# Dilated attention values as [v, ones, v] in gate stages, with one unit and several scores moved

## The chip, the cores and the metric

The kernel runs on one core of a Trainium2 chip. The metric is the device time of one execution in microseconds (us), as the median over several executions.

## The reference

Eight batches of eight heads, 576 positions, 64 elements a head. Heads 0 to 3 attend to the last 32 positions, heads 4 to 7 to every fourth of the last 128. The result is fed through a gated feed-forward block of 4608 tokens. This cut and the later ones are shortened: `...` stands for what is left out, and some comments are mine.

```python
def _attn_ref(q, k, v):
    window, dilation, scale = 32, 4, 1.0 / np.sqrt(D)
    scores = scale * np.matmul(q, k.transpose(0, 1, 3, 2))
    rel = pos[:, None] - pos[None, :]
    mask_plain = (rel >= 0) & (rel < window)
    mask_dil = (rel >= 0) & (rel < window * dilation) & (rel % dilation == 0)
    # heads 0 to 3 take mask_plain, heads 4 to 7 mask_dil
    ...
    attn = attn / (np.sum(attn, axis=-1, keepdims=True) + 1e-09)
    return np.matmul(attn, v)

def _moe_ref(x, w_gate, w_val, w_out):            # x: 4608 x 512
    g = x @ w_gate                                # 512 x 1536
    gelu = 0.5 * g * (1.0 + erf(g * inv_sqrt2))
    return gelu * (x @ w_val) @ w_out             # 1536 x 512
```

## The kernel before

The tokens go through the feed-forward block in 9 chunks of 512. A chunk is a gate stage, 12 blocks `nb` of 8 matmuls (`ffn1`), and an output stage, 4 blocks `tb` of 12 matmuls (`ffn2`). The attention of later batches is put between these matmuls. Its unit is a pair of heads of one batch: unit n belongs to batch n // 4, and units 22, 23, 26, 27, 30 and 31 are the dilated ones of batches 5 to 7. A unit consists of scores (TensorE), an exponential (ScalarE), a mask (VectorE), values (TensorE) and a normalization (VectorE). All of it goes through the four PSUM banks (PSUM is the memory that TensorE writes its results to) that the feed-forward matmuls leave free at that time.

The schedule is four tables. `values_a` puts the values of a unit behind block nb of a gate stage. `values_b` lists the units whose values go into an output stage, and `places` says where: "1.3v" is before matmul 3 of block 1, with s for a score, m for a mask, v for values and x for the normalizing multiply. One score also ends each gate stage of chunks 1 to 5.

```python
scores = {1: range(8, 12), 2: range(12, 17), 3: range(17, 22), 4: range(22, 27), 5: range(27, 32)}
values_b = {1: range(8, 12), 2: range(12, 16), 3: range(17, 20), 4: range(22, 24), 5: range(27, 28)}
values_a = {3: {4: 16}, 4: {2: 20, 6: 21}, 5: {1: 24, 4: 25, 7: 26}, 6: {1: 28, 4: 29, 7: 30, 10: 31}}
places = {
    ...
    2: "0.0m 1.3v 1.3s 1.3x 1.3m 2.5v 2.5s 2.5x 2.5m 3.0s 3.0m 3.6v 3.6x 3.7s 3.12w 3.12m",
    3: "0.0m 1.3v 1.3s 1.3x 1.3m 2.5v 2.5s 2.5x 2.5m 2.11s 2.11m 3.4s 3.6v 3.6x 3.6m",
    4: "0.0m 1.3v 1.3s 1.3x 1.3m 2.4v 2.4s 2.4x 2.4m 2.11s 2.11m 3.7s 3.7m",
    5: "0.0m 1.3v 1.3s 1.3x 1.3m 2.1s 2.1m 2.10s 2.10m 3.6s 3.6m",
}
```

A plain unit in a gate stage uses value tiles in which a block of ones lies between the values of two heads. A 128-column slice [v, ones] or [ones, v] then gives the numerator of a head in one half of the partitions and its denominator in the other half, with full-width matmuls. The price is on VectorE: the two heads lie in different banks and different halves, so each step of the normalization is done twice on 64 partitions.

```python
def emit_both(n, b0):                       # plain units in gate stages
    for hl in range(2):
        for j in range(5):
            trio = vp[:, j, hp] if j < 4 else vt[:, hp]          # [v, ones, v]
            nc.tensor.matmul(ps[:, b0 + 2 * hl + j // 4, ...],
                             trio[:, hl : hl + 2, :].rearrange("p x d -> p (x d)"), pt[:, hl, p0 : p0 + w], ...)

def norm_both_x(n, b0):
    for hl in range(2):
        half = slice(64 * hl, 64 * hl + 64)
        nc.vector.tensor_tensor(xT[pair(n)][half, ...], both_rows(hl, b0, hl), rb[half], ALU.mult)
```

A dilated unit, wherever it stands, takes the other form (`emit_pv`). Its denominators (ones as weights) and its numerators are separate half-width matmuls, and one transpose and one multiply on 128 partitions normalize it. The multiply also puts the four classes of positions back in order, by a permuted access pattern:

```python
num = ps[:, b0 + flip : b0 + flip + 2, 0 : 2 * NCL].rearrange("p s (m i) -> p i m s", m=2)
nc.vector.tensor_tensor(dst.rearrange("p (i m s) -> p i m s", m=2, s=2), num,
                        rb.rearrange("p (s m i) -> p i m s", s=2, m=2), ALU.mult)
```

The dilated values of a batch come in three DMAs on the software queue of GpSimd (`load_v_dil`). The keys and queries of a plain pair come through transposing DMAs into `qTp`. Chunk c loads those of batch c + 2, and their first score can stand in the same chunk: unit 28, the first of batch 7, has its score in chunk 5.

The softmax here doesn't subtract the row's maximum and nothing guards it: scores larger than these inputs give would overflow.

Of the kernel before, what the change touches and what calls it, by code (L numbers as in the profile page):

```python
# [21 lines left out]
def kernel(  # L22
# [10 lines left out]
    nc = tc.nc  # L33
# [23 lines left out]
    psum = ctx.enter_context(tc.tile_pool(name="psum", bufs=1, space=bass.MemoryType.PSUM))  # L57
    ldp = ctx.enter_context(tc.tile_pool(name="ldp", bufs=1))
    qtp = ctx.enter_context(tc.tile_pool(name="qtp", bufs=2))
    prb = ctx.enter_context(tc.tile_pool(name="prb", bufs=8))  # L60
    nrm = ctx.enter_context(tc.tile_pool(name="nrm", bufs=2))
    ffn = ctx.enter_context(tc.tile_pool(name="ffn", bufs=3))
    osbp = ctx.enter_context(tc.tile_pool(name="osbp", bufs=4))
# [11 lines left out]
    wo_t = [const.tile([P, 4, DM], F16, tag=f"wo{i}", name=f"wo{i}") for i in range(3)]  # L75
    xT = [const.tile([P, NT], F16, tag=f"xT{i}", name=f"xT{i}") for i in range(NKC)]

    HP = HK // 2
    vset = [
        (  # L80
            const.tile([P, 4, HP, 3, D], F16, tag=f"vp{i}", name=f"vp{i}"),
            const.tile([P, HK, 4, D], F16, tag=f"vd{i}", name=f"vd{i}"),
            const.tile([P, HP, 3, D], F16, tag=f"vt{i}", name=f"vt{i}"),
            const.tile([P, HK, 2, D], F16, tag=f"vr{i}", name=f"vr{i}"),
        )
        for i in range(3)
    ]
# [57 lines left out]
    def load_wo(i):  # L145
        return nc.gpsimd.dma_start(
            out=wo_t[i], in_=moe_w_out[i * CH : (i + 1) * CH, :].rearrange("(fc p) m -> p fc m", p=P)
        )

    tiles = {}  # L150
    gate = {}

# [9 lines left out]
    def fl(t):  # L162
        return t.rearrange("p h r d -> p h (r d)")
# [23 lines left out]
    def new_v(b):  # L187

        sv = ldp.tile([P, 5, HK, D], F32, tag="sv", name=f"sv{b}")
        tiles["v", b] = vset[b % 3]  # L190
        return sv

    def v_plain(b, sv, eng):
        for kb in range(5):
# [38 lines left out]
    def load_eights(b):  # L233
# [4 lines left out]
            )  # L238
        return q8

    def load_v_dil(b):
        nc.gpsimd.dma_start(out=fl(tiles["v", b][1]), in_=quads(v, b, HK, 0, 4 * P))
        load_v_dil_rest(b)

    def load_v_dil_rest(b):
        for m in range(2):
            nc.gpsimd.dma_start(
                out=fl(tiles["v", b][3][64 * m : 64 * m + 64]),
                in_=quads(v, b, HK, S - 256, S)[:, :, 2 * m * D : 2 * m * D + 2 * D],
            )  # L250

    def load_batch_plain(b):
        st = load_qk_plain(b)
# [31 lines left out]

    def is_plain(n):
        return pair(n) < NHP // 2

    def copy(eng, dst, src):
        if eng == "act":  # L290
# [105 lines left out]
    def emit_pv(n, b0, parts=("den", "num"), wide=False, flip=False):  # L396



        b, hp = n // NHP, n % 2  # L400
        vp, vd, vt, vr = tiles["v", b]
        pt = tiles["P", n]
        mms = []

        def add(hl, c0, dims, lhs, p0, pdims, st):

            base = ps[64 * hl : 64 * hl + 64, b0 + c0 // 512, c0 % 512 : c0 % 512 + 1]
            o = bass.AP(tensor=base.tensor, offset=base.offset, ap=[base.ap[0]] + dims)
            rhs = bass.AP(tensor=pt.tensor, offset=pt.offset + p0, ap=[pt.ap[0]] + pdims)
            mms.append((o, lhs, rhs, st))  # L410

        def run(n):
            return [[1, n]]

        if is_plain(n):
            if "den" in parts:
                d0 = 1024 if wide else 0 if flip else 960

                groups = (
                    ((0, 0, 4, P), (P, P, 3, 32), (PH - PT, 512, 1, PT))  # L420
                    if wide or flip
                    else ((0, 0, 1, 64), (64, 64, 1, 64), (PW, P, 3, P), (P, P, 3, 32), (PH - PT, 512, 1, PT))
                )
                for i, (p0, q0, runs, w) in enumerate(groups):
                    for hl in range(2):
                        st = i == 0 or i == (2 if wide or flip else 1)
                        add(hl, d0 + q0, [[P, runs], [1, w]], ones[:, 0:D], hl * PH + p0, [[PW, runs], [1, w]], st)
            if "num" in parts:
                for j in range(5):
                    for hl in range(2):  # L430
                        lhs = vp[:, j, hp, 2 * hl, :] if j < 4 else vt[:, hp, 2 * hl, :]
                        w = (PW, PW, PW, P, PT)[j]
                        p0 = hl * PH + j * PW - (32 if j == 4 else 0)
                        if not flip:
                            add(hl, j * P, run(w), lhs, p0, run(w), j in (0, 4))
                        elif j > 0:
                            add(hl, 960 + j * P, run(w), lhs, p0, run(w), False)
                        else:
                            add(hl, 960, run(64), lhs, p0, run(64), True)
                            add(hl, 1024, run(PW - 64), lhs, p0 + 64, run(PW - 64), True)  # L440
        else:
            if "den" in parts:

                groups = (
                    ((0, 0, DW, 1024), (1, 0, DW, 1536))
                    if wide
                    else ((0, 0, 192, 288), (0, 192, 96, 800), (1, 0, 96, 896), (1, 96, 192, 1312))
                )
                for i, (s, c, w, c0) in enumerate(groups):
                    for hl in range(2):  # L450
                        add(hl, c0, run(w), ones[:, 0:D], (2 * s + hl) * DW + c, run(w), wide or i != 2)
            if "num" in parts:
                for s in range(2):
                    for m in range(3):
                        for hl in range(2):
                            h, p0 = 2 * hp + hl, (2 * s + hl) * DW
                            if m < 2:
                                lhs, c0 = vd[:, h, 2 * m + s, :], 512 * (s + flip) + m * NCL
                                add(hl, c0, run(P), lhs, p0 + m * NCL, run(P), m == 0)
                            else:  # L460
                                two = [[NCL, 2], [1, 16]]
                                add(hl, 512 * (s + flip) + P, two, vr[:, h, s, :], p0 + P, two, False)
        for o, lhs, rhs, st in mms:
            nc.tensor.matmul(o, lhs, rhs, start=st, stop=True, skip_group_check=True)  # L464

    def emit_both(n, b0):


        b, hp = n // NHP, n % 2
        pt = tiles["P", n]  # L470
        vp, _, vt, _ = tiles["v", b]
        for hl in range(2):
            for j in range(5):
                w = (PW, PW, PW, P, PT)[j]
                p0 = j * PW - (32 if j == 4 else 0)
                trio = vp[:, j, hp] if j < 4 else vt[:, hp]
                nc.tensor.matmul(
                    ps[:, b0 + 2 * hl + j // 4, j % 4 * P : j % 4 * P + w],
                    trio[:, hl : hl + 2, :].rearrange("p x d -> p (x d)"),
                    pt[:, hl, p0 : p0 + w],  # L480
                    start=j in (0, 4),
                    stop=True,
                    skip_group_check=True,
                )

    def both_rows(half, b0, hl):
        return psf[64 * half : 64 * half + 64, (b0 + 2 * hl) * 512 : (b0 + 2 * hl) * 512 + S]
# [1 line left out]
    def norm_both_r(n, b0):  # L489
        dt = nrm.tile([P, 18, 32], F32, tag="dt", bufs=1)  # L490
        for hl in range(2):
            nc.vector.transpose(  # L492
                dt[64 * hl : 64 * hl + 64].rearrange("p b c -> p (b c)"), both_rows(1 - hl, b0, hl)
            )
        recip(n, dt)

    def norm_both_x(n, b0):
        b = n // NHP
        rb = tiles.pop(("rb", n))
        for hl in range(2):  # L500
            half = slice(64 * hl, 64 * hl + 64)
            nc.vector.tensor_tensor(  # L502
                xT[pair(n)][half, b * S : (b + 1) * S], both_rows(hl, b0, hl), rb[half], ALU.mult
            )

    def den_ap(n, b0, wide, flip):

# [197 lines left out]
    last_keys(0, 0, 2)  # L705
    last_keys(0, 2, HK, nc.gpsimd)
    w1 = load_w(1)[1]
    copy("pool", tiles["v", 0][1], r4(first_vd))

    dt0, dt1 = (den(n, -2 * n, t.rearrange("p (b c) -> p b c", c=32)) for n, t in enumerate(first_t))  # L710
    recip(0, dt0)
# [23 lines left out]
    for hp in range(2):  # L735
# [6 lines left out]

    mm0 = 0

    scores = {1: range(8, 12), 2: range(12, 17), 3: range(17, 22), 4: range(22, 27), 5: range(27, 32)}
    values_b = {1: range(8, 12), 2: range(12, 16), 3: range(17, 20), 4: range(22, 24), 5: range(27, 28)}
    values_a = {3: {4: 16}, 4: {2: 20, 6: 21}, 5: {1: 24, 4: 25, 7: 26}, 6: {1: 28, 4: 29, 7: 30, 10: 31}}
    biased = (9,)


# [1 line left out]

    places = {
        1: "0.0m 1.3v 1.3s 1.3x 1.3m 2.5v 2.5s 2.5x 2.5m 3.0s 3.0m 3.6v 3.6x 3.12w",
        2: "0.0m 1.3v 1.3s 1.3x 1.3m 2.5v 2.5s 2.5x 2.5m 3.0s 3.0m 3.6v 3.6x 3.7s 3.12w 3.12m",
        3: "0.0m 1.3v 1.3s 1.3x 1.3m 2.5v 2.5s 2.5x 2.5m 2.11s 2.11m 3.4s 3.6v 3.6x 3.6m",
        4: "0.0m 1.3v 1.3s 1.3x 1.3m 2.4v 2.4s 2.4x 2.4m 2.11s 2.11m 3.7s 3.7m",
        5: "0.0m 1.3v 1.3s 1.3x 1.3m 2.1s 2.1m 2.10s 2.10m 3.6s 3.6m",
    }
    places = {c: [(int(w[0]), int(w[2:-1]), w[-1]) for w in p.split()] for c, p in places.items()}  # L760
    late = False
    for c in range(NCH):
# [13 lines left out]
        for nb in range(NNB):  # L776
# [4 lines left out]
            elif nb > 1 or not (c < 2 or late):  # L781
                ffn1(c, nb, pairs[nb % 2])
            if pend is not None:
                (norm_both_x if is_plain(pend) else norm_x)(pend, SB)
                pend = None
            if nb in pv_at:
                pend = pv_at[nb]
                if is_plain(pend):
                    emit_both(pend, SB)
                    norm_both_r(pend, SB)  # L790
                else:
# [136 lines left out]
```

## Time and profile before

| | before |
|---|---|
| time, median of 4 runs | 349.02 us (348.76 to 349.36) |
| span of the profiled execution | 347.3 us |
| start and chunk 0 | 61.9 us |
| chunks 1 to 8 | 36.88, 38.12, 37.36, 37.02, 36.40, 33.95, 31.16, 34.53 us |

The lengths of the chunks are worked out from the trace: from the first gate matmul of one chunk to that of the next, and for chunk 8 to the end. Chunk 7 has no attention, so 31.16 us is a chunk at TensorE's own pace. What the others have above it is attention and waits (chunk 8 also has the end of the kernel).

### The profile page before, as it was taken

How to read it: one execution, taken by the hardware profiler on the slowest of the kernel's cores; microseconds unless marked ns; L12 is line 12 of the kernel's file. 1: busy time of each engine (PE TensorE's matmuls, PEld its weight loads, DVE VectorE, ACT ScalarE, POOL GpSimd, SP SyncE). 2: the span in 40 equal slices, each digit the busy share in tenths (PEclk: the TensorE clock that was granted, in tenths of full speed). 3: DMA queues.
4: the chain of work that ended last, by engine and by line, in shares of the span. 5: the costliest groups of instructions: out<-in, count | busy, mean ns of one | idle time of the engine just before them, and what ended most of it. 6: DMA issues, size and time to landing. Idle time of an engine off the chain costs nothing.

```text
span 347.3 us, 6004 instructions
## 1 busy us (share of the span) xinstructions
PE 335.7 (97%) x2342; PEld 163.3 (47%) x2342; DVE 202.1 (58%) x309; ACT 147.9 (43%) x220; POOL 82.2 (24%) x121
## 2 busy tenths in 40 slices
PE   8879999999999999999999999999999999999996
PEld 3544454444544444444544454445444444444443
DVE  3874488543793369674778676975398423303320
ACT  1753473535543446336553547236623223323321
POOL 8693304630630630243006300420000000000000
PEclk9999999999999999999999999999999999999999
DMA  8999999999999993897169924891100020020002
GB/s 176 227 202 225 200 201 181 184 153 272 195 142 273 194 143 101 183 175 121 63 157 170 149 79 130 183 145 49 74 2 0 32 91 1 2 90 30 2 30 91
DMA packets 106460, 44.44 MB, mean 128 GB/s; under 512 B 83296, under 2 KB 101856, under 8 KB 106432
## 3 DMA queue, kind: packets, MB, share of 16 engines
q1 hardware_dynamic: 84192, 31.01, 40.7%
q0 software_dynamic: 21696, 12.33, 27.4%
q10 hardware_dynamic: 544, 0.72, 0.8%
q8 instruction: 18, 0.29, 0.4%
q14 instruction: 10, 0.08, 0.1%
HBM read 39.85 MB, written 9.44 MB: 142 GB/s over the span
## 4 chain that ended last, share of the span: by engine, by line
PE 71%; DVE 12%; DMA 10%; issue 3%; ACT 2%; POOL 1%; SPq 1%; DVEq 0%; POOLq 0%; ACTq 0%
PE ps L576 42%; PE ps L610 21%; PE ps L464 4%; DMA st<-in_k_dram 4%; DMA sv<-in_v_dram 3%; DMA wv<-in_moe_w_val_dram 3%; DVE dt L492 2%; DVE u_all L599 2%; DVE dt L525 2%; DVE rb L536 1%; DVE P L392 1%; DVE xT L551 1%; DVE xT L502 1%; PE ps L382 1%; PE ps L352 1%
## 5 line engine op out<-in xcount | busy, mean ns | idle before, releaser
L599 DVE SCALAR_TENSOR_TENSOR u_all<-g,ps 128x512 f16<-128x512 f16 x108 | 72.8, 684 | 76.3 <-PE ps L576 67.9
L598 ACT ACTIVATE g<-ps 128x512 f16<-128x512 f32 x108 | 63.9, 596 | 123.4 <-PE ps L576 122.9
L576 PE MATMUL ps<-xT,wg 128*128 128x512 f16 x432 | 114.0, 379 | 0.8 <-POOL xT L699 0.4
L576 PE MATMUL ps<-xT,wv 128*128 128x512 f16 x432 | 113.8, 379 | 0.8 <-DMA wv<-in_moe_w_val_dram 0.6
L610 PE MATMUL ps<-wo,u_all 128*128 128x512 f16 x420 | 97.2, 380 | 0.2 <-DVE qTd L295 0.2
L576 PEld LDWEIGHTS <-wv 128*128 128x128 f16 x432 | 42.3, 98 | 53.0 <-issue 1.6
L576 PEld LDWEIGHTS <-wg 128*128 128x128 f16 x432 | 41.3, 98 | 48.7 <-issue 1.1
L610 PEld LDWEIGHTS <-u_all 128*128 128x128 f16 x420 | 38.4, 98 | 44.4 <-issue 0.8
L621 ACT ACTIVATE osb<-ps 128x512 f32<-128x512 f32 x33 | 19.7, 598 | 40.0 <-PE ps L610 39.9
L220 POOL CAST qp<-st 128x2048 f16<-128x2048 f32 x6 | 11.4, 1893 | 103.5 <-DMA sv<-in_v_dram 59.0
L536 DVE STREAM_TRANSPOSE rb<-rc 128x576 f32<-128x576 f32 (+4 forms) x34 | 25.3, 743 | 1.3
L525 DVE STREAM_TRANSPOSE dt<-ps 128x576 f32<-128x576 f32 x21 | 16.3, 778 | 13.2 <-PE ps L464 13.0
L384 ACT ACTIVATE P<-ps 128x1152 f16<-128x1152 f32 x16 | 18.1, 1130 | 12.0 <-PE ps L382 12.0
L362 ACT ACTIVATE P<-ps 128x960 f16<-128x960 f32 x16 | 15.5, 970 | 10.4 <-PE ps L352 10.3
L551 DVE TENSOR_TENSOR xT<-ps,rb 128x576 f16<-128x576 f32 x16 | 17.9, 1131 | 2.2 <-PE ps L464 1.9
L392 DVE TENSOR_TENSOR P<-P,mask_d 128x1152 f16<-128x1152 f16 x13 | 9.8, 750 | 9.7 <-ACT P L384 9.7
L392 DVE TENSOR_TENSOR P<-P,mask_p 128x1344 f16<-128x1344 f16 x14 | 11.8, 856 | 2.9 <-ACT P L363 2.9
L464 PE MATMUL ps<-P,ones 128*64 128x96 f16 (+5 forms) x174 | 11.2, 244 | 2.2 <-DVE P L392 1.5
L464 PEld LDWEIGHTS <-ones 128*64 128x64 f16 x174 | 7.0, 109 | 11.6 <-issue 8.8
L623 DVE TENSOR_SCALAR osb<-ps 128x512 f32<-128x512 f32 x2 | 1.4, 691 | 18.2 <-PE ps L610 18.2
L204 POOL CAST vp<-sv 128x1024 f16<-128x1024 f32 x8 | 8.5, 1065 | 12.8 <-DMA sv<-in_v_dram 12.8
L492 DVE STREAM_TRANSPOSE dt<-ps 64x576 f32<-64x576 f32 x14 | 10.9, 781 | 0.4
(86 smaller groups left out, 247.0 us busy)
## 6 DMA issues: line engine op xcount, KB each, us to landing
out_dram<-osb SPq DMA_DIRECT2D x35, 256.0 KB, 2.0
sv<-in_v_dram SPq DMA_DIRECT2D x40, 128.0 KB, 3.5
st<-in_q_dram SPq DMA_DIRECT2D x24, 128.0 KB, 3.0
st<-in_k_dram SPq DMA_DIRECT2D x24, 128.0 KB, 3.7
vd<-in_v_dram POOLq DMA_DIRECT2D x7, 256.0 KB, 6.3
wg<-in_moe_w_gate_dram POOLq DMA_DIRECT2D x3, 512.0 KB, 7.4
wv<-in_moe_w_val_dram POOLq DMA_DIRECT2D x3, 512.0 KB, 10.3
wo<-in_moe_w_out_dram POOLq DMA_DIRECT2D x3, 512.0 KB, 20.0
```

Of the source, the lines that this page charges most:

```text
L384: nc.scalar.activation(pt, ps[:, b0 : b0 + 4, 0:DW], AF.Exp, bias=0.0, scale=scale)
L392: nc.vector.tensor_tensor(pt, pt, mb, ALU.mult)
L464: nc.tensor.matmul(o, lhs, rhs, start=st, stop=True, skip_group_check=True)
L492: nc.vector.transpose(dt[64 * hl : 64 * hl + 64].rearrange("p b c -> p (b c)"), both_rows(1 - hl, b0, hl))
L525: nc.vector.transpose(dst, den)
L536: nc.vector.transpose(rb[:, 0 : 32 * nb].rearrange("p (b c) -> p b c", c=32), bass.AP(tensor=rc.tensor, offset=rc.offset, ap=[rc.ap[0], [1 ...
L551: nc.vector.tensor_tensor(dst.rearrange("p (i m s) -> p i m s", m=2, s=2), num, rb.rearrange("p (s m i) -> p i m s", s=2, m=2), ALU.mult,)
L576: nc.tensor.matmul(ps[:, bank, :], w[:, kc, ns], xT[kc][:, tok], start=first, stop=end)
L598: nc.scalar.activation(g, ps[:, banks[0], :], AF.Gelu)
L599: nc.vector.scalar_tensor_tensor(u_all[:, nb, :], g, USCALE, ps[:, banks[1], :], ALU.mult, ALU.mult)
L610: nc.tensor.matmul(ps[:, bank, :], u_all[:, fc, tb * P : (tb + 1) * P], wo_t[fc // 4][:, fc % 4, :], start=(fc == 0), stop=(fc == NNB - 1),)
L621: nc.scalar.activation(osb, ps[:, bank, :], AF.Copy, bias=0.0, scale=1.0 / USCALE)
```

## The change

The intent is to take the half-width form out of the gate stages altogether. (1) The dilated value tiles become [v, ones, v] too and are used so for batches 5 to 7, with 12 full-width matmuls instead of 16 half-width ones. (2) Unit 22, which stood in an output stage, moves to the gate stage of chunk 4. (3) Scores and values are put side by side in chunks 2 and 3, so that TensorE changes its mode (full-width, half-width or score matmuls) less often. (4) The new tiles need twelve smaller loads a batch instead of three, and one buffer for probabilities less.

```diff
-    prb = ctx.enter_context(tc.tile_pool(name="prb", bufs=8))
+    prb = ctx.enter_context(tc.tile_pool(name="prb", bufs=7))
...
-            const.tile([P, HK, 4, D], F16, tag=f"vd{i}", name=f"vd{i}"),
+            const.tile([P, HP, 4, 3, D], F16, tag=f"vd{i}", name=f"vd{i}"),
...
-    values_a = {3: {4: 16}, 4: {2: 20, 6: 21}, 5: {1: 24, 4: 25, 7: 26}, ...}
+    values_a = {3: {4: 16}, 4: {1: 20, 4: 21, 8: 22}, 5: {1: 24, 4: 25, 8: 26}, ...}
+    spread = (5, 6, 7)
...
+    def load_v(b, dst, src):
+        if b not in spread:
+            nc.gpsimd.dma_start(out=fl(side_by_side(dst)), in_=src)
+            return
+        for h in range(HK):
+            nc.gpsimd.dma_start(
+                out=dst[:, h // 2, :, 2 * (h % 2), :], in_=src[:, h, :].rearrange("p (r d) -> p r d", d=D))
...
+    def in_one(n):
+        return n in all_at and (is_plain(n) or n // NHP in spread)
...
 def emit_both(n, b0):
+            else:                                          # dilated
+                for s in range(2):
+                    o = ps[:, b0 + 2 * hl + s, 0:DW].rearrange("p (m i) -> p m i", m=2)
+                    src = pt[:, 2 * s + hl, :].rearrange("p (m i) -> p m i", m=2)
+                    for m in range(2):
+                        mm(o[:, m, 0:P], vd[:, hp, 2 * m + s], src[:, m, 0:P], hl, m == 0)
+                    mm(o[:, :, P:NCL], vr[:, hp, s], src[:, :, P:NCL], hl, False)
...
 def norm_both_x(n, b0):                                    # for each hl, 64 partitions
+                num = ps[half, b0 + 2 * hl : b0 + 2 * hl + 2, 0:DW].rearrange("p s (m i) -> p i m s", m=2)
+                nc.vector.tensor_tensor(dst.rearrange("p (i m s) -> p i m s", m=2, s=2), num,
+                                        rb[half].rearrange("p (s m i) -> p i m s", s=2, m=2), ALU.mult)
...
-    scores = {..., 3: range(17, 22), 4: range(22, 27), 5: range(27, 32)}
-    values_b = {..., 3: range(17, 20), 4: range(22, 24), 5: range(27, 28)}
+    scores = {..., 3: range(17, 23), 4: range(23, 28), 5: range(28, 32)}
+    values_b = {..., 3: range(17, 20), 4: range(23, 24), 5: range(27, 28)}
...
-        2: "... 3.0s 3.0m 3.6v 3.6x 3.7s 3.12w 3.12m",
-        3: "0.0m 1.3v 1.3s 1.3x 1.3m 2.5v 2.5s 2.5x 2.5m 2.11s 2.11m 3.4s 3.6v 3.6x 3.6m",
-        4: "0.0m 1.3v 1.3s 1.3x 1.3m 2.4v 2.4s 2.4x 2.4m 2.11s 2.11m 3.7s 3.7m",
-        5: "0.0m 1.3v 1.3s 1.3x 1.3m 2.1s 2.1m 2.10s 2.10m 3.6s 3.6m",
+        2: "... 3.0s 3.0m 3.6v 3.6s 3.6x 3.12w 3.12m",
+        3: "0.0m 0.6s 0.6m 1.5v 1.5s 1.5x 1.5m 2.4v 2.4s 2.4x 2.4m 2.11s 2.11m 3.6v 3.6s 3.6x 3.6m",
+        4: "0.0m 1.3v 1.3s 1.3x 1.3m 2.1s 2.1m 2.10s 2.10m 3.6s 3.6m",
+        5: "0.0m 1.3v 1.3s 1.3x 1.3m 2.3s 2.3m 3.1s 3.1m",
```

## The prediction

> **What bounds the kernel now.** I read the page's busy shares first, then the chain that ended last, then the groups, then the timeline around each attention block. "Gate stage" is the first half of a chunk (12 blocks of 8 matmuls, L576), "output stage" the second (4 blocks of 12, L610); a unit is one pair of heads of one batch, 32 in all.
>
> ```profile
> PE 335.7 (97%) x2342; PEld 163.3 (47%) x2342; DVE 202.1 (58%) x309; ACT 147.9 (43%) x220; POOL 82.2 (24%) x121
> ```
> TensorE is busy 97% of the span at full clock. In chunk 7, which has no attention, the chain shows 96 gate matmuls in 20.80 us, 216.7 ns each. So the time is the matmuls' pace plus what each attention block inserts, plus the waits where TensorE stands still. I measured the insertions as: start of the next feed-forward matmul, less start of the last one before, less 217 ns.
>
> ```profile
> 267.94 1.03 PE L576 MATMUL ps<-xT,wv 128*128 128x512 f16 x4
> 268.90 0.44 PE L464 MATMUL ps<-P,ones 128*64 128x288 f16 x4
> 269.54 0.82 PE L576 MATMUL ps<-xT,wg 128*128 128x512 f16 x3
> ```
> This is the values of dilated unit 31 in a gate stage, in half-width (64-column) matmuls that run in pairs. The last gate matmul starts at 268.59, so the block inserts 0.95 - 0.22 = 0.73 us. The same subtraction gives 0.58 for a plain unit in the [v, ones, v] form (10 full-width matmuls, 1344 columns), 0.74 for dilated values alone in an output stage, 0.47 for dilated scores, 0.49 for plain scores, 1.11 for dilated values with dilated scores directly behind, 1.14 with plain scores.
>
> TensorE also waits, mostly for VectorE:
> ```profile
> 261.41 1.51 DVE L502 TENSOR_TENSOR xT<-ps,rb 64x576 f16<-64x576 f32 x2
> 262.96 1.29 DVE L599 SCALAR_TENSOR_TENSOR u_all<-g,ps 128x512 f16<-128x512 f16 x2
> 262.98 0.44 PE L464 MATMUL ps<-P,ones 128*64 128x288 f16 x4
> ...
> 203.08 1.13 DVE L551 TENSOR_TENSOR xT<-ps,rb 128x576 f16<-128x576 f32 x1
> 204.13 0.75 DVE L392 TENSOR_TENSOR P<-P,mask_d 128x1152 f16<-128x1152 f16 x1
> 204.93 0.44 PE L464 MATMUL ps<-P,ones 128*64 128x192 f16 x8 [0.61 <-DVE P L392]
> ```
> Above, unit 30 waits until unit 29's normalization has left the shared PSUM banks: its block inserts 0.95 instead of 0.73. Below, in chunk 4, unit 23's values wait 0.68 us for the mask that VectorE reaches only after unit 22's normalization.
>
> ```profile
> L525 DVE STREAM_TRANSPOSE dt<-ps 128x576 f32<-128x576 f32 x21 | 16.3, 778 | 13.2 <-PE ps L464 13.0
> L551 DVE TENSOR_TENSOR xT<-ps,rb 128x576 f16<-128x576 f32 x16 | 17.9, 1131 | 2.2 <-PE ps L464 1.9
> L492 DVE STREAM_TRANSPOSE dt<-ps 64x576 f32<-64x576 f32 x14 | 10.9, 781 | 0.4
> L502 DVE TENSOR_TENSOR xT<-ps,rb 64x576 f16<-64x576 f32 x14 | 10.5, 748 | 0.1
> ```
> The reader should see that 64 partitions cost VectorE what 128 do (781 against 778 ns), and that the dilated, permuted multiply (L551) costs 1131.
>
> **What the Trainium skill says.** "TensorEngine Tiling (Array Packing)", Key Properties: changing the tiling mode drains TensorE. The trace agrees: the step from a gate matmul to the first half-width one is 309 ns instead of 217, 92 ns. "VectorE: DVE Perf Modes", Why `tensor_reduce` can't reduce along partition axis: each partition lane is an independent pipeline; hence the equal times above. "DMA: Bandwidth & Descriptors", Specifications: below 512 B a transfer misses line rate. The trace's packets of the value loads on the software queue take 60 to 80 ns at 512 B and 41 at 256 B, so smaller ones cost more per byte. The same page, Queues, rings and completion order: an engine takes turns between its queues. The trace shows something harsher, below.
>
> **The change part by part.**
> 1. Dilated units 26, 30, 31 stay in gate stages and take the new form: 12 full-width matmuls instead of 16 half-width ones. Columns 4 x (128+128+32) = 1152, 0.48 us; with about 3 ns each and a floor near 26 ns for the four short ones, an estimate of 0.55, and no mode switch. Against 0.73 that is -0.18 each.
> 2. Unit 22 leaves an output stage for chunk 4's gate stage; its scores move to chunk 3, and later scores follow (chunk 3 has 6 scores, chunks 4 and 5 have 5 and 4).
> 3. Chunk 2: the score at 3.7 moves next to the values at 3.6. One mode switch less, 0.09, and the last value block, which waited 0.32 us for that score's exponential, starts about 0.3 earlier. In all -0.3.
> 4. Chunk 3, insertions with waits before: 0.49 + 1.25 + 1.20 + 0.49 + 0.80 + 0.74 = 4.97. After: 0.49 + 0.47 + 1.25 + 1.14 + 0.49 + 1.11 = 4.95 for one more score. But unit 18's score now comes 6 matmuls (1.3 us) behind unit 17's, in the same banks. Before, unit 17's exponential (behind a 1.28 us table load) ended at 161.46 while TensorE would be there at 160.75; with 0.37 us of work split over two releases this is a wait of about 0.6. Values 18 wait perhaps 0.1. So +0.7.
> 5. Chunk 4 before: 2 x 0.58 + 0.47 + 1.22 + 1.82 + 0.49 + 0.47 = 5.63. After: 2 x 0.58 + 0.55 + 0.47 + 1.24 + 0.49 + 2 x 0.47 = 4.85. The 0.68 wait is gone, but there is a new one. VectorE's work for a dilated unit grows from 0.78 + 0.27 + 0.78 + 1.13 = 2.96 us to 2 x 0.78 + 0.27 + 0.78 + 2 x 1.13 = 4.87. After a gate-stage value block the trace has the reciprocal's transpose end 3.1 us behind the next gate matmul's start and a gate product at 3.7; two multiplies then end at 6.0. The score at the end of the stage needs those banks 3 x 1.73 + 0.09 = 5.3 us after it: a wait of 0.7. Net -0.1.
> 6. Chunk 5 before: 2 x 0.58 + 0.95 + 0.47 + 1.24 + 0.49 + 2 x 0.47 = 5.25. After: 2 x 0.58 + 0.55 + 0.49 + 1.24 + 2 x 0.47 = 4.38, and the same wait of 0.7: -0.15. But the score here is now unit 28, of batch 7, whose keys are loaded in this very chunk (next part).
> 7. Chunk 6: unit 30's wait nearly goes (-0.35 with the new form). Unit 31 comes three blocks behind unit 30, where VectorE has 4.87 + 3 x 0.65 of work: its multiplies end about 269.65, TensorE asks at 268.5. Half of the block can go at 268.5, the rest waits 0.9. With a small wait at the last gate product, +0.35 net.
> 8. Loads of batches 5 to 7: 12 software-queue DMAs instead of 3, each over 64 elements. By the issue times (769 and 632 ns) and the descriptors, GpSimd spends some 6 us more a batch, which it has. The packets rise from 1024 to 3072, an estimate of 31 to 41 ns each, so 6 to 8 us of all 16 engines instead of 3.3.
>
> Without the last part's effect the sum is -0.3 + 0.7 - 0.1 - 0.15 + 0.35 = +0.5 us.
>
> ```profile
> L276 SPq DMA_TRANSPOSE qTp<-qp x5: 1199/1257/1265, 118.3 to 123.5; - x5
> DMA to landing us min/median/max: 2.5/3.7/7.0
> ...
> L276 SPq DMA_TRANSPOSE qTp<-qp x5: 1200/1257/1346, 226.9 to 232.2; - x5
> DMA to landing us min/median/max: 2.4/4.3/6.0
> ```
> These are the transposing loads of the plain queries and keys, in chunk 2 (above) and 5. In chunk 2 the last took 7.0 us, because query and key loads of the software queue ran just then; in chunk 5 the first took 6.0 and its packets began only when the value loads were nearly through. In chunk 5 the last lands at 234.64. After the change TensorE asks for it at 211.29 + 20.8 + 1.72 + 0.09 = 233.9, and the bank wait lasts to 234.6, so even without slower loads there is no slack. With 3 to 4 us more traffic ahead of these loads I expect 1 to 3 us of added wait, though half of the twelve DMAs come too late to be in the way. I count +1.7. All together +2.2, 351.1.
>
> **The rivals.**
> (a) TensorE's work is what matters and VectorE catches up: the saved 0.18 x 3, the mode switches and the lost waits of chunks 2, 3, 4 and 5 come through, and the new waits are smaller than my ledger. For it: 97% busy TensorE, and placements that look deliberately moved to leave VectorE room (26 from block 7 to 8). Against: the old trace already shows TensorE waiting for VectorE in blocks 1 to 7. It would make 346.5 to 348.5.
> (b) The batch 7 transposes are late by the full added traffic: chunk 5 stands still 4 us or more, 353 to 355. For it: the 7.0 us above. Against: smaller packets may let the transposes in between.
> (c) The added loads matter to GpSimd or to chunk 4 too (unit 24's score now comes 28 us into the chunk; its keys landed at 25 before): another 1 to 2 us.
>
> **Range and chances.** The ledger says 351.1; since somebody placed these blocks with care, I give (a) about a third and settle at 350.2. Executions agree within 0.2%, so the range is my uncertainty in the waits: 347.5 to 353.2. Two per cent is 7 us, more than any rival gives.
>
> **What would show it.** Right: value groups of 12 full-width matmuls inserting about 0.55; the permuted multiply on 64 partitions at about 1131 ns; waits of some 0.7 before the scores at the ends of gate stages 4 and 5 and 0.9 within unit 31; a longer one before unit 28's score, ended by a DMA of qTp. Wrong: no DMA wait there, or multiplies on 64 partitions near 750 ns, which would bring the time below 348.

## More of the kernel before

All the executions that are compared here are fast: the granted TensorE clock was 0.97 to 1.00 of full speed in each of them.

The prediction shows the busy shares, the groups and the timelines. Two more lines of the view of TensorE's waits (who waited for whom: us in total, times, the longest) tell where this kernel stood still for VectorE:

```profile
PE ps L464 <- DVE P L392: 1.5, 4, 0.6
...
PE ps L576 <- DVE u_all L599: 0.2, 1, 0.2
```

The first is values waiting for a mask. The second is the only wait of this kernel for the product that empties the gate banks.

## The result, and the profile after

The changed kernel takes 350.26 us (349.64 to 350.47, 4 runs) against 349.02 us. The ratio is 1.0032, with a 95% interval of 1.0015 to 1.0049. Here and below a ratio is the mean time of one kernel's fast runs over the mean of the other's of the same rounds, so it is not quite the ratio of the medians. The kernel is a little slower, by a third of a per cent.

The chunks in the two traces, beside the terms of the prediction:

| chunk | before | after | difference | predicted |
|---|---|---|---|---|
| 1 | 36.88 | 36.83 | -0.05 | 0 |
| 2 | 38.12 | 37.76 | -0.36 | -0.3 |
| 3 | 37.36 | 38.21 | +0.85 | +0.7 |
| 4 | 37.02 | 37.39 | +0.37 | -0.1 |
| 5 | 36.40 | 36.34 | -0.06 | -0.15, and +1.7 for loads |
| 6 | 33.95 | 34.75 | +0.80 | +0.35 |
| 7 and 8 | 65.69 | 65.68 | -0.01 | 0 |
| sum | 285.42 | 286.97 | +1.55 | +0.5, and +1.7 |

The sum of the traces says +1.55 us and the times say +1.24. The part ahead of chunk 1 was 0.5 us shorter in this trace of the changed kernel, within its variation.

The busy shares and the groups (line, engine, operation, count | busy us, mean ns of one | idle before) of the changed kernel:

```profile
PE 336.6 (97%) x2322; PEld 163.9 (47%) x2322; DVE 210.2 (60%) x317; ACT 148.1 (43%) x220; POOL 102.0 (29%) x154
...
L602 DVE TENSOR_TENSOR xT<-ps,rb 128x576 f16<-128x576 f32 x12 | 13.4, 1134 | 2.2 <-PE ps L497 1.9
L550 DVE TENSOR_TENSOR xT<-ps,rb 64x576 f16<-64x576 f32 x8 | 8.9, 1116 | 0.1
```

TensorE has 20 instructions less and VectorE is busy 8.1 us longer. The four units in the new form (22, 26, 30, 31) have eight multiplies on 64 partitions (L550). Each takes 1116 ns, as long as one on 128 partitions (L602). TensorE's busy time does not show the gain (336.6 us, 335.7 before), so I go by the insertions: in the new form a unit takes 0.55 us of TensorE where nothing holds it up, against 0.73 in the old one.

The view of TensorE's waits, the lines that are new:

```profile
PE ps L509 <- DVE xT L550: 0.7, 1, 0.7
PE ps L627 <- DVE u_all L650: 0.5, 2, 0.3
PE ps L415 <- DVE xT L550: 0.5, 1, 0.5
PE ps L385 <- DVE xT L550: 0.5, 1, 0.5
PE ps L415 <- ACT P L395: 0.3, 1, 0.3
PE ps L415 <- ACT P L396: 0.2, 1, 0.2
```

L509 is the values in the new form, L415 and L385 are scores (dilated and plain), and L627 is the gate matmuls. Four of the six lines name VectorE, and three of those the new multiply. One of the two waits in the L627 line, 0.23 us in chunk 2, is the one of before. The timeline (start, us) shows where each stands. First the ends of the gate stages of chunks 4 and 5, where the score of unit 23 and that of unit 28 come three blocks behind the values of units 22 and 26:

```profile
195.83 2.26 DVE L550 TENSOR_TENSOR xT<-ps,rb 64x576 f16<-64x576 f32 x2
...
198.14 0.27 PE L415 MATMUL ps<-qTd 64*128 64x128 f16 x3 [0.46 <-DVE xT L550]
...
232.65 2.27 DVE L550 TENSOR_TENSOR xT<-ps,rb 64x576 f16<-64x576 f32 x2
...
234.96 0.45 PE L385 MATMUL ps<-qTp 64*128 64x160 f16 x9 [0.45 <-DVE xT L550]
```

The scores start when the second multiply has ended, at 198.1 and 234.9. Their blocks insert 1.13 and 1.17 us, where the same scores alone insert 0.47 and 0.49: both waits are 0.67 us (the 0.46 in brackets is only the idle time behind the first matmul of the group).

Unit 31 stands three blocks behind unit 30:

```profile
267.73 2.27 DVE L550 TENSOR_TENSOR xT<-ps,rb 64x576 f16<-64x576 f32 x2
...
268.89 0.27 PE L509 MATMUL ps<-P,vd 128*128 128x128 f16 x2
...
270.05 0.27 PE L509 MATMUL ps<-P,vd 128*128 128x128 f16 x2 [0.73 <-DVE xT L550]
```

The first head of unit 31 starts when the first multiply of unit 30 has left its two banks, and the second head when the second one has. The block inserts 1.60 us instead of 0.55, so the wait is 1.05.

Chunk 4, behind units 20 and 21, plain units that now stand behind blocks 1 and 4:

```profile
190.03 1.28 DVE L650 SCALAR_TENSOR_TENSOR u_all<-g,ps 128x512 f16<-128x512 f16 x2
...
190.77 1.02 PE L627 MATMUL ps<-xT,wv 128*128 128x512 f16 x4 [0.27 <-DVE u_all L650]
```

By the insertions there are two waits. The values of unit 21, behind block 4, wait 0.28 us until unit 20's multiplies have left the banks. The one shown stands in block 8, where a gate matmul waits 0.43 us because VectorE comes to its products only after unit 21's multiplies (188.49 to 190.00). In chunk 5 units 24 and 25 stand behind the same blocks, and only 0.16 us are lost, in block 8. There VectorE's first product starts 2.8 us after the start of the stage, and 3.7 in chunk 4, whose first two blocks are interleaved; this may be why, but no run tests it.

Chunk 3, the score of unit 18:

```profile
159.19 0.97 ACT L395 ACTIVATE P<-ps 128x960 f16<-128x960 f32 x1
160.06 0.48 ACT L396 ACTIVATE P<-ps 128x384 f16<-128x384 f32 x1
...
160.21 0.21 PE L415 MATMUL ps<-qTd 64*128 64x128 f16 x1 [0.30 <-ACT P L395]
...
160.59 0.27 PE L415 MATMUL ps<-qTd 64*128 64x128 f16 x3 [0.17 <-ACT P L396]
```

Unit 18's score needs the banks that unit 17's exponential still reads. It is released in two steps, and the block inserts 1.20 instead of 0.47 us, a wait of 0.73. Chunk 3 has another wait of 0.21 us at 3.6, within the values of unit 19. By the times of the trace they waited for ScalarE to copy out the output block before them (171.39 to 171.99), which it did late, behind unit 21's exponential.

Last the loads, in the totals of the queue (packets, MB, share of 16 engines' span) and in the view of the transposing loads and the value loads of batch 7 in chunk 5:

```profile
q0 software_dynamic: 28272, 12.33, 30.5%
```
```profile
L305 SPq DMA_TRANSPOSE qTp<-qp x5: 1193/1258/1880, 226.5 to 232.4; - x5
...
DMA to landing us min/median/max: 2.3/3.9/5.4
...
L268 POOL DMA_DIRECT2D vd<-in_v_dram x4: 742/744/767, 223.5 to 225.7; - x4
...
DMA to landing us min/median/max: 4.9/5.2/5.8
```

The software queue had 21696 packets and 27.4% before. The new packets of 128 bytes take 32 ns each, and each of the four value loads landed within 5.8 us of its issue, where the one of four times the size had taken 7.8. The last transposing load landed at 234.67 us, 0.03 later than before (chunk 5 itself began 0.29 later), and the score that needs it started at 234.96, when the multiply (234.92) had let it go anyway.

### The profile page after: what moved, and what is told of

It is laid out like the page before. It is cut to its first block, busy times and chain, and to the rows that moved or that the text cites. A ratio compares the mean times of both kernels' runs of the same rounds, so it can differ in the third digit from the quotient of the medians.

```text
span 348.4 us, 6007 instructions
## 1 busy us (share of the span) xinstructions
PE 336.6 (97%) x2322; PEld 163.9 (47%) x2322; DVE 210.2 (60%) x317; ACT 148.1 (43%) x220; POOL 102.0 (29%) x154
## 3 DMA queue, kind: packets, MB, share of 16 engines
q0 software_dynamic: 28272, 12.33, 30.5%
## 4 chain that ended last, share of the span: by engine, by line
PE 71%; DVE 11%; DMA 10%; issue 3%; ACT 3%; SPq 1%; POOL 1%; DVEq 0%; POOLq 0%; ACTq 0%
PE ps L627 41%; PE ps L661 22%; DMA st<-in_k_dram 4%; PE ps L497 3%; DMA sv<-in_v_dram 3%; DMA wv<-in_moe_w_val_dram 3%; DVE u_all L650 2%; DVE dt L537 1%; DVE dt L576 1%; DVE xT L550 1%; PE ps L509 1%; PE ps L415 1%; DVE rb L587 1%; DVE P L425 1%; DVE xT L602 1%
## 5 line engine op out<-in xcount | busy, mean ns | idle before, releaser
L627 PE MATMUL ps<-xT,wv 128*128 128x512 f16 x432 | 113.8, 379 | 1.1 <-DMA wv<-in_moe_w_val_dram 0.6
L627 PE MATMUL ps<-xT,wg 128*128 128x512 f16 x432 | 114.0, 379 | 0.7 <-POOL xT L750 0.4
L627 PEld LDWEIGHTS <-wv 128*128 128x128 f16 x432 | 42.2, 98 | 53.7 <-issue 2.6
L627 PEld LDWEIGHTS <-wg 128*128 128x128 f16 x432 | 41.2, 98 | 48.1 <-issue 0.8
L576 DVE STREAM_TRANSPOSE dt<-ps 128x576 f32<-128x576 f32 x17 | 13.2, 778 | 9.5 <-PE ps L497 9.3
L602 DVE TENSOR_TENSOR xT<-ps,rb 128x576 f16<-128x576 f32 x12 | 13.4, 1134 | 2.2 <-PE ps L497 1.9
L268 POOL DMA_DIRECT2D vr<-in_v_dram x24 | 14.1, 596 | 1.5 <-DMA vd<-in_v_dram 1.4
L497 PE MATMUL ps<-P,ones 128*64 128x96 f16 (+5 forms) x154 | 9.6, 241 | 1.1 <-DVE P L425 0.8
```

The source lines that it names most:

```text
L497: nc.tensor.matmul(o, lhs, rhs, start=st, stop=True, skip_group_check=True)
L576: nc.vector.transpose(dst, den)
L627: nc.tensor.matmul(ps[:, bank, :], w[:, kc, ns], xT[kc][:, tok], start=first, stop=end)
```

## The experiments

My theory after the result: the loads are free, the new form gains its 0.18 us of TensorE a unit and loses more through the second multiply on VectorE, which comes before the next user of the four banks; the new places of chunk 3 lose on their own. Rivals: that it is the places and not the form; that it is the loads; or that it is the work on TensorE and not VectorE's. Each set of runs had its own runs of the kernel before: 349.01 us (first four), 348.99 (second four), 348.92 (last four), 11 runs each. The lengths of chunks 1 to 8 together are in this table; the last column is the part that moved.

| kernel | time, us | ratio to before | chunks 1 to 8, us | against the kernel after, by chunk |
|---|---|---|---|---|
| before | 348.9 to 349.0 | 1 | 285.42 | |
| after | 350.26 | 1.0032 | 286.97 | |
| e1, form alone | 350.44 | 1.0044 | 287.00 | 2: +0.32, 3: -0.85, 4: -0.36, 5: +0.92 |
| e3, loads alone | 349.03 | 0.9998 | 285.30 | as before |
| e8, chunk 2 alone | 349.05 | 1.0009 | 285.02 | as before but 2 |
| e5, as e6, with 3 output tiles | 369.35 | 1.0581 | 304.83 | 1: +19.69, 4: -0.74, 5: -0.44, 6: -0.75 |
| e2b, places alone | 349.37 | 1.0016 | 285.53 | 4: -0.48, 5: -0.19, 6: -0.81 |
| e4, one multiply | 349.02 | 1.0001 | 284.82 | 4: -0.68, 5: -0.52, 6: -1.14, 8: +0.20 |
| e6, ScalarE and GpSimd | 348.13 | 0.9978 | 284.99 | 4: -0.67, 5: -0.56, 6: -0.71 |
| e7, chunk 3 later | 349.89 | 1.0030 | 286.26 | 3: -0.65 |
| e9, e6 with e7 | 347.31 | 0.9964 | 284.68 | 3: -0.66, 4: -0.67, 5: -0.22, 6: -0.72 |
| e10, e9 with units 20 and 21 moved | 347.50 | 0.9971 | 284.49 | 3: -0.66, 4: -0.60, 5: -0.47, 6: -0.72 |
| e11, old form, places of e10 | 349.45 | 1.0023 | 285.19 | 3: -0.66, 4: -0.74, 5: +0.40, 6: -0.81 |

### Taking the change apart

**e1_form_only.** The changed kernel with all tables of the kernel before.

```diff
-    values_a = {3: {4: 16}, 4: {1: 20, 4: 21, 8: 22}, 5: {1: 24, 4: 25, 8: 26}, ...}
+    values_a = {3: {4: 16}, 4: {2: 20, 6: 21}, 5: {1: 24, 4: 25, 7: 26}, ...}
     (scores, values_b and places likewise)
```

> The changed kernel with the placements, scores and value lists of the kernel before: only the [v, ones, v] form of units 26, 30 and 31 and its loads are new. My theory (VectorE's norm of a dilated unit grew by 1.9 us and TensorE waits for it): chunk 6 stays at its 34.75 us of the changed kernel (33.95 before), chunk 5 loses about what it gains, so 349.7 to 350.2. Rival 1 (TensorE's work is what matters, the form saves 0.18 us a unit): 348.4 to 348.7. Rival 2 (the new placements alone cost the time): 348.9 to 349.1.

It took 350.44 us (350.18 to 350.83), ratio 1.0044 (1.0031 to 1.0057), above what I had expected. So the form alone costs as much as the whole change. The places are not needed for the loss: chunks 2 to 4 are within 0.04 us of the kernel before, chunk 5 is 0.86 longer than before and chunk 6 0.80. In chunk 5, with unit 26 still behind block 7, the gate matmuls wait 1.19 us for VectorE's late products by the insertion (the line counts 1.0 for it; the other of its two waits, 0.23 us in chunk 2, is that of the kernel before):

```profile
PE ps L627 <- DVE u_all L650: 1.3, 2, 1.0
```

In the changed kernel, with unit 26 behind block 8, chunk 5 has no such wait. (It also has one score less than here, so the 0.92 us between the two is not this wait alone.)

**e3_loads_only.** e1 with the old matmuls on the new tiles, so that only the twelve loads, the ones, the layout and the one buffer less for probabilities are left.

```diff
     (tables as in e1)
-        return n in all_at and (is_plain(n) or n // NHP in spread)
+        return n in all_at and is_plain(n)
```

> The kernel before in matmuls and placements, but with the changed kernel's layout, memsets and twelve loads a batch for batches 5 to 7. By the changed kernel's trace (the last transposing load of batch 7 lands as early as before, small packets 32 ns) the loads are free: within 0.2 us of before. The prediction's rival (loads delay the transposes into chunk 4 or 5): 350 or more.

349.03 us (348.69 to 349.14), ratio 0.9998 (0.9986 to 1.0010), and every chunk within 0.06 us of the kernel before. The loads are free. The rival of the loads falls, and with it the largest term of my prediction.

**e2_schedule_only.** The changed kernel with the old form and loads, so that the places alone are left.

```diff
-    spread = (5, 6, 7)
+    spread = ()
```

> The changed kernel with the set of spread batches empty: old half-width form and old loads, new placements, unit 22 in a gate stage in the old form. My theory: the waits of 0.7 us before the scores that end gate stages 4 and 5 go, as VectorE needs 3.0 us instead of 4.9 for a dilated unit; chunk 6 is back at 33.95; only chunk 3 stays longer by 0.85 and chunk 2 shorter by 0.36: 348.2 to 348.9, below the changed kernel by 1.4 to 2. Rival 2 (the placements cost the time): 350.0 or more.

Five fast executions took 349.03 to 350.41 us, ratio 1.0018 (1.0004 to 1.0032); I had expected a gain. A sixth one, the profiled one, took 692.85 us and was counted as slow. Its trace has TensorE at half its pace from start to end (443 ns from one matmul to the next at the median, 215 in the trace of the kernel before), at a recorded granted clock of 1.00; I have no explanation for it, and the trace is of no use for this comparison.

**e2b_schedule_again.** The same edit.

> The same kernel as e2_schedule_only, whose profiled execution took 692.85 us and shows nothing; its other five took 349.0 to 350.4. Wanted is its trace. My theory, after that result: chunk 3 is 0.8 longer and chunk 2 0.36 shorter as in the changed kernel; the waits of 0.7 before the scores at the ends of gate stages 4 and 5 are not there; chunk 6 is at 33.95. If so the sum is near 349.0, unless chunks 4 and 5 hold a wait that I have not seen. Rival: the waits at the ends of the gate stages are there in the old form too.

349.37 us (349.00 to 350.67, 6 runs), ratio 1.0016 (1.0002 to 1.0031). In its trace the places alone cost 0.11 us: chunk 2 gains 0.34, chunk 3 loses 0.85, chunk 4 gains 0.11 and chunk 5 0.25. The times say 0.38 by the medians, but 0.35 of it lies outside the span from the first to the last instruction: time less span is 2.03 to 2.10 us in this kernel and 1.68 to 1.74 in the one before. There is no wait for the multiply at the ends of gate stages 4 and 5. The waits behind units 20 and 21 (0.28 and 0.43 us) are there all the same: they come from putting units 20 and 21 behind blocks 1 and 4, not from the form. And the score of unit 28 waits 0.29 us for its keys, as the chain that ended last shows:

```profile
233.63 2.31 DMA qTp<-qp
...
235.98 0.20 PE ps L385 x2
```

So the place of this score has no room before its keys, with the old loads too. In the changed kernel the wait for the multiply hides it.

**e8_chunk2_only.** The kernel before with the new places of chunk 2.

```diff
-        2: "... 3.0s 3.0m 3.6v 3.6x 3.7s 3.12w 3.12m",
+        2: "... 3.0s 3.0m 3.6v 3.6s 3.6x 3.12w 3.12m",
```

> The kernel before with the changed kernel's placements in chunk 2 alone (the score at 3.7 goes behind the values at 3.6). Chunk 2 took 37.76 us instead of 38.12 in the changed kernel; alone it should give the same: 348.5 to 348.8. Rival (the gain of chunk 2 is given back in the next chunk, whose start waits for VectorE): 348.9 to 349.1.

349.05 us (348.04 to 350.67), ratio 1.0009 (0.9991 to 1.0028): in time it is inconclusive. In the trace chunk 2 takes 37.77 us instead of 38.12 and no later chunk gives that back.

### VectorE's second multiply

**e4_one_multiply.** One permuted multiply on 128 partitions in place of the two on 64. It reads the wrong banks for half of the partitions, so the result is wrong (relative error 151.5); the times of the other instructions don't depend on it.

```diff
 def norm_both_x(n, b0):
+        if not is_plain(n):
+            nc.vector.tensor_tensor(
+                xT[pair(n)][:, b * S : (b + 1) * S].rearrange("p (i m s) -> p i m s", m=2, s=2),
+                ps[:, b0 : b0 + 2, 0:DW].rearrange("p s (m i) -> p i m s", m=2),
+                rb.rearrange("p (s m i) -> p i m s", s=2, m=2), ALU.mult)
+            return
```

> The changed kernel with one permuted multiply over 128 partitions instead of two over 64 for the dilated units of gate stages; wrong result on purpose (the upper half reads the wrong bank). It takes 1.13 us of VectorE a unit away and nothing else. My theory: the waits before the scores that end gate stages 4 and 5 (0.67 each) go, the wait of 1.05 within unit 31 shrinks to near nothing: 348.1 to 348.8, 1.5 to 2.1 below the changed kernel. Rival (the waits are set by the transposes, the loads or the placements): within 0.4 of the changed kernel, 349.9 to 350.4.

349.02 us (348.45 to 349.33), ratio 1.0001 (0.9988 to 1.0013). That is 1.2 us below the changed kernel but just misses the range I gave. In the trace the waits went nearly as expected: the score of unit 23 inserts 0.47 us, that of unit 28 0.65 (0.15 of it for its keys), and unit 31 0.73, so that 0.18 of its wait of 1.05 is left. Chunks 1 to 8 are 2.15 us shorter, although the last store ended 0.20 us later behind the last matmul, which I can't explain. By the times the gain is 1.2 us only; the rest would have to lie ahead of chunk 1, where one trace can't show it. In e2b, which has the old form in the same places, units 22 and 26 insert 0.73 us each where they insert 0.55 here: the 0.18 that the form was made for is there at these two once VectorE does no second multiply. Unit 30 inserts 0.60 instead of 0.94, part of it a shorter wait for the banks, and unit 31 inserts 0.73 in both. (The sums of chunks 1 to 8 differ by 0.71, near 4 x 0.18, but that is a coincidence.)

**e5_act_pool.** A correct way to take the multiply from VectorE: ScalarE copies the two numerators out of PSUM, which frees the banks, and GpSimd multiplies from there. The copy needs room, which I took from the output tiles.

```diff
-    osbp = ctx.enter_context(tc.tile_pool(name="osbp", bufs=4))
+    osbp = ctx.enter_context(tc.tile_pool(name="osbp", bufs=3))
 def norm_both_r(n, b0):
+        if not is_plain(n):
+            nm = nrm.tile([P, S], F32, tag="nm", bufs=1)
+            for hl in range(2):
+                nc.scalar.copy(nm[half]..., ps[half, b0 + 2 * hl : b0 + 2 * hl + 2, 0:DW])
+            tiles["num", n] = nm
 def norm_both_x(n, b0):
+        if not is_plain(n):
+            nc.gpsimd.tensor_tensor(xT[pair(n)]..., nm (permuted), rb (permuted), ALU.mult)
+            return
```

> The changed kernel, but for dilated units in gate stages ScalarE copies the numerators out of PSUM and GpSimd multiplies, so that VectorE only transposes and takes reciprocals (2.6 us instead of 4.9). To make room the output tiles have 3 buffers instead of 4. My theory: the waits of 0.7 (chunks 4 and 5), of 1.05 and 0.26 (chunk 6) go: 348.0 to 348.5, and it may beat the kernel before by 0.5 to 1. Rival (these waits are for something else, or ScalarE now delays the gate products): 349.5 or more.

369.35 us (368.22 to 370.40), ratio 1.0581. The waits of TensorE and of ScalarE say why:

```profile
PE ps L643 <- ACT osb L688: 18.0, 1, 18.0
...
ACT osb L688 <- DMA out_dram<-osb: 22.2, 2, 21.3
```

With three output tiles instead of four, ScalarE waited 21.3 us for a store to leave a tile in chunk 1, and TensorE with it. It is a side effect of my edit and tells nothing of the change. The chunks that matter spoke for the idea all the same: 4 to 6 took 106.55 us together, against 108.48 in the changed kernel and 107.37 before.

**e6_act_pool_4.** The same with four output tiles. The copies go into the tile of the additive masks, which has no use after the start.

```diff
-    bias_p = const.tile([P, PH], F16, tag="bias_p")
-    bias_d = const.tile([P, DW], F16, tag="bias_d")
+    bias = const.tile([P, 2 * S], F16, tag="bias")
+    bias_p, bias_d = bias[:, 0:PH], bias[:, PH : PH + DW]
...
+            nm = bias.bitcast(F32)
```

> As e5_act_pool, with 4 output buffers again; the copies go to the place of the bias tiles, which are dead by then. e5 lost 20 us in chunk 1 to its missing output buffer, but its chunks 4 to 6 took 106.55 us against 108.48 of the changed kernel and 107.37 of the kernel before. Expected: chunk 1 back at 36.8, the rest as in e5: 348.2 to 348.6. Rival (the 1.9 us came from the lower granted clock or the shifted loads of that run): 349.5 or more.

348.13 us (347.66 to 348.83), ratio 0.9978 (0.9966 to 0.9990), with a right result. It beats both kernels. Its groups and the timeline at unit 31:

```profile
L552 POOL TENSOR_TENSOR xT<-bias,rb 128x576 f16<-128x576 f32 x4 | 8.8, 2204 | 34.2 <-DVE rb L603 34.2
L542 ACT COPY bias<-ps 64x576 f32<-64x576 f32 x8 | 5.1, 634 | 9.6 <-DVE dt L537 9.3
```
```profile
267.62 0.28 PE L509 MATMUL ps<-P,vd 128*128 128x128 f16 x2
...
267.90 0.27 PE L509 MATMUL ps<-P,vd 128*128 128x128 f16 x2
```

The second head of unit 31 now follows 0.28 us behind the first, where it was 1.16 in the changed kernel. GpSimd needs 2204 ns for its multiply, twice VectorE's time, but no bank waits for it. Together with e4 this shows the cause of what the form loses: the second multiply in front of the next user of the banks, and not anything on TensorE. The loss of chunk 3 (0.85) is another matter and stays in both; e7 is about it.

### Chunk 3

**e7_chunk3_later.** The score of unit 18 and the block at 3.6 come later.

```diff
-        3: "0.0m 0.6s 0.6m 1.5v ... 3.6v 3.6s 3.6x 3.6m",
+        3: "0.0m 0.9s 0.9m 1.5v ... 3.7v 3.7s 3.7x 3.7m",
```

> The changed kernel with two placements of chunk 3 moved: unit 18's score from matmul 6 to 9 of its block (its exponential then is done), and the values of unit 19 with the score of unit 22 from 6 to 7 of the last block (ScalarE's eviction is then done). If the two waits that the trace shows there (0.73 and 0.21) are the cause of chunk 3's extra 0.85: chunk 3 falls from 38.2 to 37.3 to 37.6 and the time by 0.6 to 0.9, to 349.4 to 349.7. Rival (one more score in chunk 3 is what costs): no change.

349.89 us (349.70 to 350.67), ratio 1.0030 (1.0018 to 1.0042). That is 0.37 us less than the median of the changed kernel's own rounds, where I expected 0.6 to 0.9; by the times the two can't be told apart. In the trace chunk 3 takes 37.56 instead of 38.21 us, and the other chunks are the same within 0.06. The score of unit 18 starts at once,

```profile
160.81 0.37 PE L415 MATMUL ps<-qTd 64*128 64x128 f16 x4
```

and the values of unit 19 have no wait (1.11 us with the score behind them, 1.32 in the changed kernel). A new wait of 0.20 us at the end of the stage is what is left. This agrees with the two waits being for ScalarE; for the second one it remains an inference.

### Putting it together

**e9_both.** e6 and e7 in one, no further edit.

> e6_act_pool_4 and e7_chunk3_later together. They touch different chunks, so their gains against the changed kernel should add, 2.1 and 0.4 to 0.65: 347.4 to 347.8. Rival (they share a wait): 348.0 or more.

347.31 us (347.06 to 348.23), ratio 0.9964 (0.9949 to 0.9978): the fastest kernel, 1.6 us under the kernel before. The score of unit 28 waits 0.38 us for its keys here, which is why chunk 5 gains less than in e6.

**e10_all_moved.** e9 with unit 20 back behind block 2 and unit 21 behind block 5, against the waits behind units 20 and 21.

```diff
-    values_a = {3: {4: 16}, 4: {1: 20, 4: 21, 8: 22}, ...}
+    values_a = {3: {4: 16}, 4: {2: 20, 5: 21, 8: 22}, ...}
```

> e9_both with units 20 and 21 at blocks 2 and 5 of chunk 4 instead of 1 and 4. In the changed kernel, with the old form and with ScalarE and GpSimd alike, two waits of 0.28 and 0.43 stand behind unit 20 at block 1, which comes while VectorE still has the mask of the last output stage. If VectorE's start of that chunk is the cause, they go: 346.7 to 347.2. Rival (three blocks between 20 and 21 are too few wherever they lie): no better than e9.

347.50 us (347.43 to 349.04), ratio 0.9971 (0.9956 to 0.9986): no better than e9, against what I expected. The two waits went, but 0.26 us came back at the start of the stage and 0.50 for a `g` that ScalarE wrote late behind its copies. Chunk 4 takes 36.79 us, 36.72 in e9.

**e11_old_form_moved.** The old form with the places of e10, to see what the form itself is worth in a good schedule.

```diff
-    spread = (5, 6, 7)
+    spread = ()
     (values_a and places as in e10; VectorE multiplies)
```

> The placements of e10, but the old half-width form and the old loads for dilated units. It says what the [v, ones, v] form is worth once VectorE is no longer in its way: by TensorE's insertions 4 x 0.18 and the wait of 0.2 before unit 30, so e10 should be 0.6 to 1.0 faster than this: 347.5 to 348.1. Rival (the form is worth nothing even then): equal to e10 within 0.2.

349.45 us (349.23 to 350.28), ratio 1.0023 (1.0011 to 1.0035), above the 347.5 to 348.1 that I expected. e10 is 1.9 us faster by the medians but only 0.70 us in chunks 1 to 8 of the traces. And those 0.70 are about the difference in the wait of unit 28's score for its keys, 0.13 us in e10 and here

```profile
PE ps L385 <- DMA qTp<-qp: 0.7, 1, 0.7
```

(0.87 by the insertion). Chunks 4 and 6, where three of the four units are, agree within 0.15 us, in favour of the old form. Of the rest, some 0.25 us lies outside the span of the instructions (time less span is 2.05 to 2.13 us here and 1.80 to 1.89 in e10). The last 1 us would have to lie ahead of chunk 1, which I could not settle: the one profiled execution of e10 was its slowest (349.04 us) and had the long start. So I can't say that the form is worth anything in the end with this schedule. The 0.18 us a unit are there (e4), but even with the multiply on GpSimd they are spent again on waits for ScalarE.

## Why the prediction was right or wrong

The time is right almost to a tenth (350.2 predicted, 350.26 measured), and that is largely luck. Two errors of opposite sign met: the waits were under-sized by about 1 us, and the term for the loads, +1.7, should have been zero. The 0.9 taken off for rival (a) made up most of the difference. By its own steps:

1. **The cost of the new form** (part 1: 0.55 inserted, -0.18 a unit) is right: 0.55 measured where nothing holds the unit up, and e4 against e2b gives 0.18 at each of units 22 and 26.
2. **Chunk 2** (part 3: -0.3) is right: -0.36, and the trace of e8 shows that it stays.
3. **Chunk 3** (part 4: +0.7) has the right sum, +0.85, and the right main term, a wait of 0.73 for unit 17's exponential where I had 0.6. The 0.1 for values 18 did not occur; 0.21 at unit 19 did, which I had not looked for. e7 took both away.
4. **Chunk 4** (part 5: -0.1) is wrong in sign: +0.37. The mechanism that I named is right: the wait of 0.7 in front of the score at the end of the stage measured 0.67, behind multiplies of 1116 ns where I had 1131. What failed is the step "After: 2 x 0.58 + ...", which let units 20 and 21 go in at their bare cost. They brought 0.28 + 0.43 us of waits for VectorE, because they stand one and two blocks earlier than before: with both one block later, the waits are gone (e10, and e11 with the old form). e2b shows them with the old form too, so they belong to the new places, which I had priced at nothing. A wait of 0.26 at the start of the stage that is gone gave some of it back.
5. **Chunk 5 without the loads** (part 6: -0.15) is right within 0.1: the wait is 0.67 here too, the sum -0.06; 0.16 us that a gate matmul of block 8 loses was not counted.
6. **Chunk 6** (part 7: +0.35) has the right mechanism and the wrong size: +0.80. The wait within unit 31 measured 1.05 where I had 0.9, and the "small wait at the last gate product" was 0.26 us in the first block of the output stage. By my own numbers unit 30 gives -0.35 and unit 31 0.55 + 0.9 - 0.73 = +0.72, which is the whole of the +0.35: I had named the small wait and counted nothing for it.
7. **The loads** (part 8: +1.7) failed. The sentence is "With 3 to 4 us more traffic ahead of these loads I expect 1 to 3 us of added wait". It took the landing to be set by the bytes and packets ahead. It rested on the reading that the first transposing load's packets "began only when the value loads were nearly through", and that reading was too strong: in the old trace they begin at 229.18 us, behind 576 of the 1024 value packets. In the new one they begin at 229.11, behind about half of the 3072; from there the packets of both queues run side by side, and the last load landed 0.03 us later than before. e3 with 0.9998 shows the term to be zero. The "against" of rival (b) had allowed for this ("smaller packets may let the transposes in between"), and I weighed it too little; that it is the size of the packets that did it is not shown. The other half of the same part, that there is no slack in front of unit 28's score, is right: e2b, e4 and e11 wait 0.29, 0.15 and 0.87 us there once the banks are free earlier, two of them with the old loads.
8. **Rival (a)**, that VectorE catches up, was given a third. e4 shows what it would have been worth: chunks 1 to 8 at 284.82 us, 0.6 under the kernel before, and nothing in the time (1.0001). By the chunks that is at the low edge of the 0.4 to 2.4 us that I gave it, because chunk 3's loss stays in; by the time it is outside. Rivals (b) and (c) fell with e3.

So the ledger without the loads said +0.5, the traces +1.55, and the pull of rival (a) and the term of the loads made +1.3 of it.

## What to carry to other kernels

A form that saves an engine that is busy 97% of the time can still cost time if it gives more work to the engine that clears the buffers in front of it: price the form by when the banks come free, next to who asks for them then, and not by the matmuls that it saves. When a normalization holds shared banks, copying the numbers out and letting an idle engine do the rest may be worth more than the faster matmuls; check then that the room for the copy isn't taken from a buffer that another path needs. A total that comes out right says little, so compare the terms.

## What the Trainium skill lacked or had wrong

- "VectorE: DVE Perf Modes", Mode 1x (REGULAR), counts one result a cycle in the mode that takes PSUM operands and odd strides alike, and gives no slower case. The runs differ: at 576 elements a multiply that reads PSUM in order takes 748 ns, and the permuted one 1116 on 64 and 1134 on 128 partitions. Both of its operands are permuted; no run here says which of them costs the time.
- "DMA: Bandwidth & Descriptors", Queues, rings and completion order, says that an engine takes turns between its queues, packet by packet, but not what many small packets on one queue do to the loads of another. Here the software queue went from 21696 to 28272 packets with the same bytes (those of the new loads 128 B in 32 ns, before half of them 512 B in 60 and half 256 B in 41, by the medians), and the transposing loads beside them landed at 234.67 us instead of 234.64: three times as many packets in these loads did not delay the other queue.
